# Two weight loads a step earlier, and four parts of the second matmul placed by hand

## The chip, the cores and the metric

The kernel runs on one core of a Trainium2 chip (trn2). The metric is the device time of one execution in microseconds; the median of the runs counts. "The profile" is one profiled execution of the same program, with its own time.

## The reference

Causal attention with a forget gate over 8 batches, 8 heads, 576 positions and head dimension 64, followed by a two-layer block with SiLU on 4608 tokens of width 512:

```python
scores = q @ k.T / sqrt(D)
cum = cumsum(log(clip(f, 1e-4, 1)))
scores = where(causal, -1e9, scores + cum[:, None] - cum[None, :])
x = softmax(scores) @ v            # heads side by side: 4608 x 512
h = x @ w_in                       # 512 x 2048
out = (h * sigmoid(h)) @ w_out     # 2048 x 512, float32
```

## The kernel before

All five engines' instructions stand in an order that the program writes out by hand; nothing is rescheduled. An engine issues in that order and waits on semaphores, so an instruction that waits holds up everything behind it on its engine.

**Attention.** exp(cum differences) is split: the values v are multiplied by exp(half - cum) per key (`convert_v0` for the first 128 rows of a batch, L349, and `convert_v` for the rest, L423, both on GpSimd), the ones column gives the softmax sum, and the query's factor cancels. The first 128 rows of a batch are made by `turn0` (L294, q and k turned by TensorE into a "big" PSUM buffer, copied by ScalarE for q and by VectorE for k), `scores0` (L328, exp on ScalarE, L335), `mask0` (L344, the causal mask on VectorE), `out0` (L368, times v; the reciprocal and xq on VectorE, L377 and L383) and `back0` (L398, xq transposed, copied by ScalarE into x, L399). The other 448 rows go by units of a batch and a pair of heads, two units to a pass m of the last loop: `scores` (L469, exp L474 and L480), `mask` and `mask_tail` (L486, L492), `attend` (L516, L525; reciprocal L533, xr L534) and `back` (L558, xr transposed, copied by VectorE, L561 and L564; from the fourth pass on by a DMA transpose).

**The two-layer block.** Tokens are taken in groups g: the first 128 rows of batches 0 to 3 are group 0 (512 columns), those of batches 4 and 5 group 1 (256), of 6 and 7 group 2 (256); then the rest. M1, `m1_chunk` (L577), makes one of 16 chunks of 128 hidden units of a group by four matmuls: ScalarE's tanh (`th`, L585) and VectorE's `gt` (L586) evacuate it. M2, `m2_part` (L622), is a quarter of the second matmul of a tile of 128 tokens: four matmuls of 128x512 into `po`, needing one of the four w_out loads; after the fourth, ScalarE makes `osb` (L632), of which there are four buffers, and SyncE stores it (L601).

**PSUM.** Four single-bank buffers ("big") serve `tp`, `tx`, `hp`, `po` and `dn`; a `po` holds one for its whole tile. Two double-bank buffers serve the scores.

**The order.** `fill(us)` places M1 chunks and M2 parts for about so many planned microseconds between the steps of attention; `wanted` chooses between the two (M2 only once `open2["w"]` is set), `step(kind)` places one, `at["left"]` carries the rest of a plan over. `two_more(4)` and `two_more(6)` do the first rows of two batches with fills between them. After them comes the loop over m, whose passes place fills (`slot`, `rest`) up to a planned total.

**The queues.** `load_qk0`, most of `load_v0`, `load_w_in` and `load_w_out` are issued by GpSimd, whose order is shared with its conversions and casts. SyncE issues the other loads, the DMA transposes and the stores, and starts its loads behind `after`, which waits for the second w_out load.

Of the kernel before, what the change touches and what calls it, by code (L numbers as in the profile page):

```python
# [18 lines left out]
def kernel(  # L19
# [177 lines left out]
    def load_w_in(i):  # L197
        c0, c1 = i * DFF // WQ, (i + 1) * DFF // WQ
        nc.gpsimd.dma_start(out=w_in_bf[:, :, c0:c1], in_=w_in_v[:, :, c0:c1])
# [106 lines left out]
    def ban0(b):  # L306
        sc = psc.tile([P, 2, NP, P], FP32, name="sc", tag="sc")
        for i in range(2):
            nc.tensor.matmul(  # L309
                sc[:, i, :, :].rearrange("p a t -> p (a t)"),  # L310
                lhsT=ident_bf[:, :],
                rhs=ban[:, :, :].rearrange("p a t -> p (a t)"),
                start=True,
                stop=False,
            )
        return sc

    def scores0(b, sc=None):
        t = qT0.pop(b)
        fresh = sc is None  # L320
        u = upool.tile([P, 2, NP, P], BF16, name="u", tag="u")
        u0[b] = u
        if fresh:
            sc = psc.tile([P, 2, NP, P], FP32, name="sc", tag="sc")
        for p in range(NP):
            for i in range(2):
                r = slice(i * D, (i + 1) * D)
                nc.tensor.matmul(  # L328
                    sc[:, i, p, :],
                    lhsT=kT0[b][r, p, :],  # L330
                    rhs=t[r, p, :],
                    start=fresh,
                    stop=fresh or p == NP - 1,
                )
        nc.scalar.activation(  # L335
            out=u[:, :, :, :].rearrange("p i a t -> p (i a t)"),
            in_=sc[:, :, :, :].rearrange("p i a t -> p (i a t)"),
            func=ACT.Exp,
            scale=scale,
        )  # L340
# [7 lines left out]
    def convert_v0(b):  # L348
        nc.gpsimd.tensor_tensor(  # L349
            out=v0[b][:, :, :],  # L350
            in0=vf0.pop(b)[:, :, :],
            in1=w_bf[:, 0, b * H : (b + 1) * H, None].to_broadcast([P, H, D + 1]),
            op=ALU.mult,
        )
# [215 lines left out]
    def m1_chunk(g, fc):  # L570
        w = GW[g]
        if fc == 0:
            gts[g] = gpools[g % 3].tile([P, NFC, w], BF16, name="gt", tag=f"gt{g % 3}")
        gt = gts[g]
        hp = pbig.tile([P, w], FP32, name="hp", tag="big")
        for cc in range(NCC):
            nc.tensor.matmul(  # L577
                hp[:, :],
                lhsT=w_in_bf[:, cc, fc * P : (fc + 1) * P],
                rhs=xcols(g, cc),  # L580
                start=(cc == 0),
                stop=(cc == NCC - 1),
            )
        th = tpool.tile([P, w], BF16, name="th", tag="th")
        nc.scalar.activation(out=th[:, :], in_=hp[:, :], func=ACT.Tanh, scale=0.5)  # L585
        nc.vector.scalar_tensor_tensor(  # L586
            out=gt[:, fc, :],
            in0=th[:, :],
            scalar=1.0,
            in1=hp[:, :],  # L590
            op0=ALU.add,
            op1=ALU.mult,
        )
# [10 lines left out]
    def m2_part(g, tb, part):  # L604
        gt = gts[g]
        last = g == NG - 1 and tb == GW[g] // P - 1
        if last:
            if part % 2 == 0:
                pos[g, tb] = pbig.tile([P, DM // 2], FP32, name="po", tag="big")
            m0 = part // 2 * DM // 2  # L610
            m1 = m0 + DM // 2
            fcs = range(part % 2 * NFC // 2, (part % 2 + 1) * NFC // 2)
            done = part % 2 == 1
        else:
            if part == 0:
                pos[g, tb] = pbig.tile([P, DM], FP32, name="po", tag="big")
            m0, m1 = 0, DM
            fcs = range(4 * part, 4 * part + 4)
            done = part == 3
        po = pos[g, tb]  # L620
        for fc in fcs:
            nc.tensor.matmul(  # L622
                po[:, :],
                lhsT=gt[:, fc, tb * P : (tb + 1) * P],
                rhs=w_out_bf[:, fc, m0:m1],
                start=(fc == 0),
                stop=(fc == NFC - 1),
            )
        if done:
            store(len(stores) - 3)  # L630
            osb = opool.tile([P, m1 - m0], FP32, name="osb", tag="osb")
            nc.scalar.activation(out=osb[:, :], in_=po[:, :], func=ACT.Copy, scale=0.5)  # L632
            for n, (r, b, s0) in enumerate(rows_of(g, tb)):
                t0 = b * S + s0
                q_ = nc.scalar if last and n == 1 else nc.sync
                stores.append((q_, out[t0 : t0 + r.stop - r.start, m0:m1], osb[r, :]))
# [45 lines left out]
    at = {"m1": 0, "m2": 0, "left": 0.0}  # L682
    ready: set[int] = set()
    open2 = {"w": False}
# [4 lines left out]
    def wanted(a, c):  # L689


        g1 = M1[a][0] if a < len(M1) else NG
        g2 = M2[c][0] if c < len(M2) else NG
        can1 = g1 in ready and not (M1[a][1] == 0 and g1 > g2 + lag["g"])
        can2 = open2["w"] and c < len(M2) and g2 < g1
        if can1 and can2 and lag["parts"]:
            return 2 if sum(M2_OF[:g1]) - c > lag["parts"] else 1
        if not can1 or not can2:
            return 1 if can1 else 2 if can2 else 0
        a0, c0 = begin.get(g1, (M1[a][1], c)) if M1[a][1] else (0, c)  # L700
        c1 = sum(M2_OF[:g1])
        f1 = (M1[a][1] - a0 + 0.5) / (NFC - a0)
        f2 = (c - c0 + 0.5) / max(1, c1 - c0)
        return 1 if f1 <= f2 else 2

    def step(force=0):

        a, c = at["m1"], at["m2"]
        want = wanted(a, c)
        if not want:  # L710
            return None
        g1 = M1[a][0] if a < len(M1) else NG
        g2 = M2[c][0] if c < len(M2) else NG
        can1 = g1 in ready and not (M1[a][1] == 0 and g1 > g2 + lag["g"])
        can2 = open2["w"] and c < len(M2) and g2 < g1
        kind = force if (force == 1 and can1) or (force == 2 and can2) else want
        if kind == 1:
            if M1[a][1] == 0:
                begin[g1] = (0, c)
            m1_chunk(g1, M1[a][1])  # L720
            at["m1"] += 1
            t = 4 * (GW[g1] / 2.4 + 2.5)
        else:
            m2_part(*M2[c])
            at["m2"] += 1
            t = 4 * (DM / 2.4 + 2.5)
        return t
# [20 lines left out]
    def fill(us_, least=0, ends=(0, 0)):  # L748

        left = us_ + at["left"]  # L750
        kinds = plan(left)
        kinds += [0] * (least - len(kinds))
        if any(ends) and kinds:
            if 2 not in kinds:
                kinds[0] = 2
            n1, n2 = len(kinds) - kinds.count(2), kinds.count(2)
            e0 = 1 if ends[0] else 0
            e1 = 1 if ends[1] and n2 > e0 else 0
            inner = n2 - e0 - e1
            n = n1 + inner  # L760
            mid = [2 if (x + 1) * inner // n > x * inner // n else 1 for x in range(n)]
            if inner and mid[-1] == 2 and e1 and not e0:
                mid = mid[::-1]
            kinds = [2] * e0 + mid + [2] * e1
        for k in kinds:
            t = step(k)
            if t is None:
                at["left"] = 0.0
                return
            left -= t / 1000  # L770
        at["left"] = left
# [13 lines left out]
    gpool = ctx.enter_context(tc.tile_pool(name="gpool", bufs=1))  # L785
    first_pool = tc.tile_pool(name="first", bufs=1)
    gpools = [first_pool.__enter__(), gpool, gpool]
    convert_v0(0)
    load_w_in(0)
    turn0(1, 0)  # L790
    turn0(1, 1)
    turn0(2, 0)
# [3 lines left out]
    out0(0, apart=True)  # L796
    turn0(3, 0)
    scores0(2, ban0(2))
    convert_v0(2)
    load_w_in(1)  # L800
    turn0(3, 1)
    bans = ban0(3)
    out0(1, apart=True)
# [53 lines left out]
    def two_more(b):  # L857
        for x in range(2):
            turn0(b + x, 0)
            turn0(b + x, 1)  # L860
        fill(1.2, 2)
        for x in range(2):
            scores0(b + x)
            mask0(b + x)
        fill(2.6 if b == 4 else 3.4, 3)
        out0(b)
        fill(0.6, 1)
        out0(b + 1)
        fill(0.8, 2)
        back0(b, on_act)  # L870
        fill(0.6, 1)
        back0(b + 1, on_act)
        fill(0.6, 1)

    fill(5.9)
    two_more(4)
    ready.add(1)
    fill(3.0)
    open2["w"] = True
    begin[M1[at["m1"]][0]] = (M1[at["m1"]][1], at["m2"])  # L880
    fill(6.0)
    two_more(6)
    ready.add(2)
    fill(4.2)
# [75 lines left out]
    for m in range(NQ):  # L960
# [16 lines left out]
        if m > 0:  # L977
            if m % 2 == 0:
                b = m // 2 - 1
# [79 lines left out]
```

## Time and profile before

| | us |
|---|---|
| median of 3 runs | 340.43 |
| lowest, highest | 340.33, 341.62 |
| profiled execution | 340.98 |
| its span, first to last instruction | 339.2 |
| TensorE busy | 330.6 |
| ScalarE, VectorE, GpSimd busy | 216.9, 193.6, 137.4 |

The granted TensorE clock is 1.00 throughout. Busy times are shares of the whole span; what one engine waits for in one place is read from the waits, the chain and the timeline. Line numbers of the profile before are those of the kernel before; in the changed kernel the lines behind the edit are the same up to L870.

### The profile page before, as it was taken

How to read it: one execution, taken by the hardware profiler on the slowest of the kernel's cores; microseconds unless marked ns; L12 is line 12 of the kernel's file. 1: busy time of each engine (PE TensorE's matmuls, PEld its weight loads, DVE VectorE, ACT ScalarE, POOL GpSimd, SP SyncE). 2: the span in 40 equal slices, each digit the busy share in tenths (PEclk: the TensorE clock that was granted, in tenths of full speed). 3: DMA queues.
4: the chain of work that ended last, by engine and by line, in shares of the span. 5: the costliest groups of instructions: out<-in, count | busy, mean ns of one | idle time of the engine just before them, and what ended most of it. 6: DMA issues, size and time to landing. Idle time of an engine off the chain costs nothing.

```text
span 339.2 us, 10025 instructions
## 1 busy us (share of the span) xinstructions
PE 330.6 (97%) x4132; PEld 222.4 (66%) x4132; DVE 193.6 (57%) x425; ACT 216.9 (64%) x389; POOL 137.4 (41%) x217
## 2 busy tenths in 40 slices
PE   7999899999999999999999999999999999999995
PEld 3745565577656768857766896867776676555654
DVE  4668935267567556655656865684672558334330
ACT  5766635677867767848748784875776485444431
POOL 8895417636756455454374434536060000000000
PEclk9999999999999999999999999999999999999999
DMA  8999999999999799999998969989763210001012
GB/s 151 190 185 222 182 210 155 199 236 177 156 190 236 117 215 134 163 211 151 168 178 172 142 130 175 134 168 165 148 123 66 56 37 33 31 33 64 33 62 63
DMA packets 144702, 48.00 MB, mean 142 GB/s; under 512 B 133328, under 2 KB 139728, under 8 KB 144656
## 3 DMA queue, kind: packets, MB, share of 16 engines
q1 hardware_dynamic: 115088, 36.60, 59.5%
q0 software_dynamic: 29408, 10.62, 26.6%
q8 instruction: 32, 0.52, 0.7%
q10 hardware_dynamic: 160, 0.13, 0.2%
q14 instruction: 14, 0.11, 0.1%
HBM read 36.85 MB, written 9.44 MB: 136 GB/s over the span
## 4 chain that ended last, share of the span: by engine, by line
PE 92%; ACT 2%; DVE 2%; DMA 2%; issue 1%; POOL 0%; POOLq 0%
PE hp L577 35%; PE po L622 24%; PE pr L648 12%; PE sc L469 7%; PE dn L516 6%; PE dn L525 3%; PE tp L294 2%; DMA qkb<-in_k_dram 2%; DVE u L344 1%; DVE gt L586 1%; ACT x L399 1%; PE sc L309 1%; PE sc L328 1%; ACT u L335 1%; PE tx L558 0%
## 5 line engine op out<-in xcount | busy, mean ns | idle before, releaser
L585 ACT ACTIVATE th<-hp 128x384 bf16<-128x384 f32 (+2 forms) x208 | 96.0, 469 | 78.7 <-PE hp L577 75.8
L586 DVE SCALAR_TENSOR_TENSOR gt<-th,hp 128x384 bf16<-128x384 bf16 (+2 forms) x208 | 107.1, 522 | 67.3 <-ACT th L585 58.5
L577 PE MATMUL hp<-x,w_in_bf 128*128 128x384 bf16 (+2 forms) x704 | 122.1, 321 | 1.5 <-ACT x L399 0.9
L577 PEld LDWEIGHTS <-w_in_bf 128*128 128x128 bf16 x832 | 79.4, 98 | 50.6 <-issue 1.8
L622 PE MATMUL po<-w_out_bf,gt 128*128 128x512 bf16 (+1 forms) x400 | 93.8, 371 | 0.0
L480 ACT ACTIVATE u<-sc 128x1024 bf16<-128x1024 f32 (+1 forms) x96 | 74.4, 814 | 6.4 <-PE sc L469 6.4
L622 PEld LDWEIGHTS <-gt 128*128 128x128 bf16 x400 | 37.6, 98 | 32.5 <-issue 0.2
L410 POOL CAST qkb<-qf 128x384 bf16<-128x384 f32 x32 | 16.7, 522 | 95.1 <-DMA qf<-in_q_dram 94.8
L648 PE MATMUL pr<-w_out_bf,gt 64*128 64x256 bf16 x768 | 46.0, 269 | 0.0
L158 POOL DMA_DIRECT2D qkb<-in_k_dram x56 | 43.8, 784 | 0.7 <-issue 0.7
L648 PEld LDWEIGHTS <-gt 64*128 64x128 bf16 x768 | 38.5, 94 | 2.8
L423 POOL TENSOR_TENSOR vp<-vf,w_bf 128x520 bf16<-128x520 f32 (+1 forms) x32 | 34.1, 1069 | 10.3 <-DMA vf<-in_v_dram 9.0
L632 ACT ACTIVATE osb<-po 128x512 f32<-128x512 f32 (+1 forms) x25 | 14.6, 583 | 22.6 <-PE po L622 19.5
L469 PE MATMUL sc<-qkT 64*128 64x128 bf16 (+1 forms) x640 | 27.9, 206 | 0.4 <-ACT u L480 0.3
L469 PEld LDWEIGHTS <-qkT 64*128 64x128 bf16 x640 | 19.9, 94 | 8.6 <-issue 6.5
L486 DVE TENSOR_TENSOR u<-u,tri 128x768 bf16<-128x768 bf16 x32 | 19.4, 605 | 10.5 <-ACT u L480 10.5
L474 ACT ACTIVATE ut<-sc 128x640 bf16<-128x640 f32 x32 | 22.5, 702 | 1.7 <-PE sc L469 1.3
L516 PEld LDWEIGHTS <-u 128*128 128x128 bf16 x576 | 20.6, 98 | 2.9
L516 PE MATMUL dn<-vp,u 128*128 128x65 bf16 x384 | 21.8, 194 | 0.0
L534 DVE TENSOR_TENSOR xr<-dn,rec 128x448 bf16<-128x448 f32 x32 | 20.0, 624 | 1.1
L516 PE MATMUL dn<-v,u 128*128 128x65 bf16 x192 | 20.0, 194 | 0.0
L577 PE MATMUL hp<-xt,w_in_bf 128*128 128x256 bf16 x128 | 16.6, 273 | 0.0
(72 smaller groups left out, 228.1 us busy)
## 6 DMA issues: line engine op xcount, KB each, us to landing
out_dram<-osb SPq DMA_DIRECT2D x32, 256.0 KB, 3.5
vf<-in_v_dram SPq DMA_DIRECT2D x26, 256.0 KB, 5.5
qf<-in_q_dram SPq DMA_DIRECT2D x64, 96.0 KB, 3.4
qkb<-in_k_dram POOLq DMA_DIRECT2D x56, 48.0 KB, 4.6
w_in_bf<-in_moe_w_in_dram POOLq DMA_DIRECT2D x4, 512.0 KB, 6.8
w_out_bf<-in_moe_w_out_dram POOLq DMA_DIRECT2D x4, 512.0 KB, 8.7
vf<-in_v_dram POOLq DMA_DIRECT2D x6, 256.0 KB, 10.3
qkb<-in_q_dram POOLq DMA_DIRECT2D x8, 128.0 KB, 5.5
```

The costliest lines, as they stand in the source:

```text
L158: nc.gpsimd.dma_start(out=t2[:, NR + 1 : NX, j * D : (j + 1) * D], in_=k[b, head(p, j), P:SM, :].rearrange("(c p) d -> p c d", p=P),)
L423: nc.gpsimd.tensor_tensor(out=vbf[b][r, c, :, :], in0=vst[b][c][r, :, :], in1=w_bf[r, c + 1, b * H : (b + 1) * H, None].to_broadcast([n, H ...
L469: nc.tensor.matmul(sc[:, i, o : o + q1 - q0], lhsT=kt, rhs=t[r, q0:q1], start=True, stop=True)
L474: nc.scalar.activation(out=ut[:, :, 0:3:2, :].rearrange("p k i t -> p i k t"), in_=sc[:, :, T0 : T0 + (NM + 1) * ST].rearrange("p i (k t) ...
L480: nc.scalar.activation(out=u[:, :, c * SM : c * SM + w], in_=sc[:, :, 0:w], func=ACT.Exp, scale=scale)
L516: nc.tensor.matmul(dn[:, i * NR + c - 1, :], lhsT=u[:, i, o : o + P], rhs=vals(kb, i), start=(kb == 0), stop=(kb == c),)
L534: nc.vector.tensor_tensor(out=xq[:, :, p % 2, :], in0=dn[:, :, 0:D], in1=rec[:, :, None].to_broadcast([P, NGR, D]), op=ALU.mult,)
L577: nc.tensor.matmul(hp[:, :], lhsT=w_in_bf[:, cc, fc * P : (fc + 1) * P], rhs=xcols(g, cc), start=(cc == 0), stop=(cc == NCC - 1),)
L585: nc.scalar.activation(out=th[:, :], in_=hp[:, :], func=ACT.Tanh, scale=0.5)
L586: nc.vector.scalar_tensor_tensor(out=gt[:, fc, :], in0=th[:, :], scalar=1.0, in1=hp[:, :], op0=ALU.add, op1=ALU.mult,)
L622: nc.tensor.matmul(po[:, :], lhsT=gt[:, fc, tb * P : (tb + 1) * P], rhs=w_out_bf[:, fc, m0:m1], start=(fc == 0), stop=(fc == NFC - 1),)
L648: nc.tensor.matmul(pos[g, tb][y], lhsT=gt[r, fc, tb * P : (tb + 1) * P], rhs=w_out_bf[r, fc, y * DM // 2 : (y + 1) * DM // 2], start=(half ...
```

## The change

Three edits. On GpSimd the first w_in load is issued ahead of `convert_v0(0)` instead of behind it, and the second ahead of `convert_v0(2)`. In `two_more(4)`, after `back0(5)`, the fill (which had nothing to place, since group 0's M1 was done and group 1 not yet declared ready) is replaced by one M2 part, and M2 is opened there. Between `two_more(4)` and `two_more(6)` ten steps are placed by name (seven M1 chunks, three M2 parts), the carried rest is set to zero, and the fill that follows is planned at 2.6 instead of 3.0 + 6.0 us.

```diff
+    load_w_in(0)
     convert_v0(0)
-    load_w_in(0)
     turn0(1, 0)
...
     scores0(2, ban0(2))
+    load_w_in(1)
     convert_v0(2)
-    load_w_in(1)
     turn0(3, 1)
...
         back0(b + 1, on_act)
-        fill(0.6, 1)
+        if b == 4:
+            open2["w"] = True
+            step(2)
+        else:
+            fill(0.6, 1)
 
     fill(5.9)
     two_more(4)
     ready.add(1)
-    fill(3.0)
-    open2["w"] = True
+    for kind in (1, 1, 2, 1, 1, 2, 1, 1, 1, 2):
+        assert step(kind) is not None
+    at["left"] = 0.0
     begin[M1[at["m1"]][0]] = (M1[at["m1"]][1], at["m2"])
-    fill(6.0)
+    fill(2.6)
     two_more(6)
```

TensorE's order then differs in this way (x256 and x512 are the columns of one matmul; four make a chunk or a part). Before: 7 chunks of M1 in a row behind `back0(5)`, then parts and chunks mixed, 6 parts and 10 chunks in all ahead of `two_more(6)`. After: 1 part, 2 chunks, 1 part, 2 chunks, 1 part, 3 chunks, 2 parts, 1 chunk, 1 part, 1 chunk: 6 parts and 9 chunks. The fills behind it place what follows differently: in the first pass of the loop a part more and no chunk or part between the attends and the second pass's scores; in the fourth pass one part fewer ahead of the attends, so that four chunks stand in a row there. From the fifth pass on the orders are the same.

## The prediction

> **What bounds the kernel now.** First the page's engine line:
>
> ```profile
> PE 330.6 (97%) x4132; PEld 222.4 (66%) x4132; DVE 193.6 (57%) x425; ACT 216.9 (64%) x389; POOL 137.4 (41%) x217
> ```
>
> TensorE does the same matmuls before and after, so only its idle time can move: 339.2 - 330.6 = 8.6 us, of which 3.8 us (the windows view) lie after 288 us. The built orders differ only up to about 107 us. Next, who waited for whom, TensorE alone, 38.5 to 288 us (us in total, times, longest):
>
> ```profile
> PE hp L577 <- ACT x L399: 0.9, 1, 0.9
> PE sc L469 <- ACT u L480: 0.3, 1, 0.3
> ```
>
> Little is left there. The chain of waits, 28 to 40 us, shows where the 0.9 us comes from (start, us, what):
>
> ```profile
> 29.04 0.92 ACT u L335
> ...
> 29.99 2.96 DVE u L344 x2
> 32.95 1.79 DVE gt L586 x3
> ...
> 37.78 0.59 ACT x L399
> ...
> 38.42 1.69 PE hp L577 x14
> ```
>
> VectorE sets the pace here, not TensorE: two masks, three evacuations, then the copy of the second group's x, for which its M1 waits. Last, GpSimd's timeline, and the DMA queues in the windows view (last two columns: share, GB/s):
>
> ```profile
> 10.28 1.05 POOL L349 TENSOR_TENSOR v<-vf,w_bf 128x520 bf16<-128x520 f32 x1 [0.91 <-issue]
> 11.28 0.80 POOL L199 DMA_DIRECT2D w_in_bf<-in_moe_w_in_dram  x1
> ...
> 29.89 2.51 POOL L349 TENSOR_TENSOR v<-vf,w_bf 128x520 bf16<-128x520 f32 x2 [4.04 <-DMA vf<-in_v_dram]
> ```
> ```profile
> 12.00:13.00 1.00, 1.00 (x25) 0.67 (x21) 0.93 (x5) 1.00 (x2) 0.98 (x2) 1.00 0.61 126
> 13.00:14.00 1.00, 1.00 (x26) 0.65 (x24) 0.34 (x1) 0.77 (x2) 1.00 (x2) 1.00 0.73 65
> 14.00:15.00 1.00, 1.00 (x18) 0.56 (x12) 0.74 (x2) 0.71 (x1) 0.98 (x3) 1.00 1.23 204
> ```
>
> GpSimd sits idle 0.91 us before the first conversion, and the transfers slacken between 12 and 14 us because no w_in is queued yet.
>
> **The two w_in loads.** GpSimd is free at 9.38 (7.53 + 1.85, the v loads), so the first issue (0.80) runs 9.38 to 10.18 instead of at 11.28, and the conversion still starts at 10.28, as its weights are ready at 10.14. Cost nothing; if it did start late, it has 0.45 us until out0(0)'s matmuls at 11.78. Conversion 1 comes 0.8 us earlier, w_in(1) is issued at 12.35 instead of 14.12, conversion 2 stays at 13.15. Conversion 3 still waits for its v (issued 8.45, landing 6.2 us later, 14.7), so GpSimd's later issues gain only 0.2 us. TensorE never waited for w_in. What can be gained is the slack: (204 - 126) + (204 - 65) = 217 KB at 204 GB/s, 1.06 us by which the queue's later transfers land earlier.
>
> Who needs that? Conversions 4 and 5 wait for v (4.04 us idle) and run beside the masks of 29.99: two masks take 2.96 us there, but 1.85 us (row at 52.86) beside no conversion. One us earlier, conversion 4 is over when the masks start; conversion 5 (v at 30.78 - 1.0) covers the first alone. The second takes 0.93 instead of 1.54 us: VectorE's chain is 0.6 us ahead at 32.95. Followed through the evacuations, xq, the last M1 and the copy, x is ready at about 37.94 instead of 38.37. **B: -0.45 us**; bounds 0 (no lead) and -0.75 (all waits 33 to 36.5 us, 0.67 us by their rows, and the second-order rest).
>
> GpSimd against VectorE has a rule. In these rows both slow down and neither stands still: a mask beside conversions took 1.50 us against 0.93, while the conversion beside it took 1.50 against 1.05. The Trainium skill (SBUF — State Buffer, "Who interferes with whom") says a VectorE instruction with two SBUF inputs and a GpSimd instruction that reads SBUF exclude each other, and the later one fully blocks. By it conversion 5, from 29.9, would hold both masks back to 31.9 and 32.8, B would be -0.1 and the sum +0.5. The trace does not bear a full block out: the first mask, begun 0.10 us after a conversion of 1.05 us, ended at 31.49, not at 31.88.
>
> **The first part in the gap.** TensorE ends back0(5)'s transposes at 37.48. The part (four 128x512 matmuls, 0.86 us by the row of po) needs w_out(0), landed at 24.32 + 9.0 = 33.3, and a PSUM buffer: in the built order that of chunk 13, evacuated at 36.94 + 0.62. So it runs 37.62 to 38.48, and M1 begins at 38.48 instead of 38.42. **A: -0.80 us.** The other three parts need w_out(1), (2), (3), landed at 35.9, 38.4 and 41.5; they come at 39.4, 41.1 and 43.3, cover 1.8 us or more. Fewer chunks stand between the second group's start and two_more(6), which starts about 1.4 us earlier; its q, k (45.0 at the latest) and v conversions (52.8 against a need at about 54) still hold.
>
> **What the new order makes late.** Walked with PSUM buffers as built and durations of the trace:
>
> - **C: -0.26 us.** In the first unit's piece, chunk 1 of the next head's scores waited for ScalarE (0.25 at 65.53). Now two M1 chunks instead of one precede it (0.44 more), and the wait goes. Bounds 0 and -0.41.
> - **D: +0.14 us.** The third turn0 in two_more(6) takes the buffer of an M1 chunk two tiles back; evacuation needs 1.47 us from a chunk's start (38.42 to 39.89), and 1.39 us passes. Bounds 0 and +0.3.
> - **E: +0.95 us.** After the second unit's attends the built order has no filler any more: scores (0.65 us), then back(0)'s transposes. Before, M1 and M2 (1.3 us) stood between. These are VectorE's rows before, attends ending at 71.68:
>
> ```profile
> 70.34 0.75 DVE L586 SCALAR_TENSOR_TENSOR gt<-th,hp 128x256 bf16<-128x256 bf16 x2 [0.33 <-ACT th L585]
> 71.03 0.20 DVE L533 RECIPROCAL rec<-dn 128x7 f32<-128x7 f32 x1
> ...
> 72.13 0.62 DVE L534 TENSOR_TENSOR xr<-dn,rec 128x448 bf16<-128x448 f32 x1
> ```
>
> xr is ready 1.07 us after the attends: a wait of 0.5 by itself. In the new ScalarE order an osb now stands ahead of the two th, which delays them by 0.48 (106.25 to 106.73, osb to th), the evacuations and xr likewise: 1.60 - 0.65 = 0.95. Queued behind the transposes on TensorE are the M2 part and three chunks; nobody else needs them. Bounds +0.45 and +1.1.
> - **F: +0.58 us.** In the fourth QUAD pass an M2 part ahead of the attends has gone earlier and four M1 chunks in a row (2.61 us) fill all four buffers. The attends take the first chunk's buffer, whose th waits behind three exps and the osb (103.47 + 0.48 + 0.44 + 0.39 + 0.91 + 0.58 + 0.27 = 106.54), evacuated at 107.7, wanted at 107.16. Bounds +0.2 and +0.75.
>
> From about 107 us the order is as before, dense, so the sum stays to the end: -0.80 - 0.45 - 0.26 + 0.14 + 0.95 + 0.58 = **+0.16 us**. The profiled execution took 340.98 us, span 339.2 and 1.8 around it, 0.55 above the median of the runs, 340.43. So 341.1 profiled, and 340.6 as a median.
>
> **The rivals.**
> 1. The new waits do not come (ScalarE has room to catch up, or the buffers come free sooner): A to D alone, -1.37, 339.1 us; with B and C at their far bounds 338.7. For it: in passes m = 2 on, transposes after little filler waited only 0.05 us. Against: there one chunk and no osb stood in that place.
> 2. Slower: the fifth osb. The output pool has four buffers, so the osb of E writes over the first one, whose store is the first of four queued on SyncE at 66.70, behind a transpose, landing 3.5 us later: 70.2. ScalarE wants it about 2.2 us after scores at 67.2 to 67.6, so at 69.4 to 69.8. If SyncE's chain does not come 1 us earlier with the loads, ScalarE stands 0.4 to 0.8 us with the th and exps behind it; E becomes 1.35 (B absent) and the sum +1.0: 341.4 us. It decides once the store lands after 69.4. Against: SyncE's loads start when w_out(1) has landed, which B moves too.
> 3. The w_in lead does nothing, because the load of v(3) and the queue's own latency fill the gap: B = 0, the sum +0.6, 341.0 us.
>
> **How the numbers follow.** The forecast 0.50 (its own range 340.0 to 341.2), rival 1 0.22, rival 2 0.15, rival 3 0.08, both masks held back in full by conversion 5 (B = -0.1) 0.05, 340.9 us. About 0.5%, 1.7 us, is what a measurement can tell from no change: below 338.7 lies only the far end of rival 1, with some room for a gap that I have not seen (0.11); above 342.1 only rival 2 with E and F at their upper bounds, or a wait not in the list (0.11); within, 0.78. Range: 339.0 (rival 1) to 341.8 (rival 2 with F at 0.75 and D at 0.3).
>
> **What would show it.** In the changed profile: GB/s near 200 at 12 to 14 us; conversions 4 and 5 about 1 us earlier and the second L344 near 0.93 us; a po of L622 before the first 128x256 M1 and no 0.9 us wait on x; new TensorE waits on xr at L558 near 72 us and on gt at L516 near 107 us. A wait of po on w_out, a late conversion 0, or no new wait at L558 would prove the steps wrong; a total outside 339.0 to 341.8, the sum.

## The result and the profile after

| | before | after |
|---|---|---|
| median of 6 runs, us | 340.57 | 346.35 |
| lowest, highest | 340.33, 341.62 | 344.09, 348.44 |
| profiled execution, its span | 340.98, 339.2 | 348.44, 346.7 |
| ratio, 95% interval | 1 | 1.0157 (1.0123 to 1.0191) |

The change costs 5.8 us in these runs; the profiled execution of after is the longest of its six. A second set of ten runs of after, on another occasion, had a median of 342.57 us, from 341.31 to 347.23 (ratio 1.0059, 1.0021 to 1.0098): six lie between 341.3 and 342.7, four between 344.6 and 347.2. The ratio of the second set leaves out its longest run, which lies more than 1.5% above its shortest. So the kernel has two outcomes, and what decides between them is the main thing to explain.

TensorE's waits in after (us in total, times, longest):

```profile
PE dn L516 <- ACT osb L632: 3.6, 1, 3.6
...
PE hp L577 <- DVE gt L586: 1.1, 1, 1.1
...
PE tx L558 <- DVE xr L534: 0.6, 1, 0.6
PE po L622 <- DMA w_out_bf<-in_moe_w_out_dram: 0.5, 1, 0.5
PE dn L516 <- DVE gt L586: 0.4, 1, 0.4
```

The 0.9 us wait for x and the 0.3 us wait of sc are gone, as forecast; the waits for xr and gt are there, as forecast; and above them stands one that before does not have, 3.6 us of the second unit's attends for an osb. ScalarE's timeline (start, us, instruction, idle before and who ended it) gives the reason:

```profile
68.94 0.39 ACT L480 ACTIVATE u<-sc 128x256 bf16<-128x256 f32 x1
73.26 0.60 ACT L632 ACTIVATE osb<-po 128x512 f32<-128x512 f32 x1 [3.93 <-DMA out_dram<-osb]
```

This is the fifth osb. ScalarE could begin it at 69.33; it starts when a store has landed. In before the same osb comes later and waits for its own po alone, 0.48 us:

```profile
73.19 0.60 ACT L632 ACTIVATE osb<-po 128x512 f32<-128x512 f32 x1 [0.48 <-PE po L622]
```

The chain of waits in after names the store too, here with the time of the transfer:

```profile
67.43 0.86 ACT u L480
68.30 4.88 DMA out_dram<-osb
...
74.16 0.75 DVE gt L586 x2
```

The fifth osb takes the first one's buffer, whose store was issued at 68.30 and landed at 73.17. Until then po keeps its PSUM bank, and the attends need that bank: TensorE stands from 70.28 to 73.90. What follows is seen in the windows (us, busy time of PE, PEld, DVE, ACT, POOL, then PEclk, DMA share, GB/s):

```profile
70.00:74.00 4.00, 0.38 (x14) 0.29 (x11) 0.00 (x0) 0.74 (x2) 1.09 (x2) 1.00 1.24 292
74.00:78.00 4.00, 3.16 (x48) 2.38 (x49) 2.75 (x8) 2.34 (x4) 1.27 (x3) 0.61 1.17 205
78.00:82.00 4.00, 4.00 (x33) 2.33 (x33) 1.01 (x4) 1.02 (x3) 3.20 (x6) 0.54 1.29 190
```

The second of these windows in before:

```profile
74.00:78.00 4.00, 4.00 (x47) 2.61 (x45) 2.00 (x5) 3.95 (x7) 2.57 (x5) 1.00 1.19 175
```

The granted clock, 1.00 there in before, falls behind the wait; by the clock's own records it is 0.5 from 74.84 to 81.67 us. The Trainium skill (TensorE: Matmul & The Clock Gate, Part 1) says that the clock halves after an idle window of about 3.4 us and returns after a busy one, and that the windows run freely. The length agrees: 6.83 us are two steps of 3.41, and the fall stands 68.27 us, twenty such steps, behind the clock's first record. The idle window agrees only in part. Counted in these steps, the window that ended at 74.84 began at 71.43, and TensorE was busy for 0.94 us of it, behind the wait.

Step by step along the units, by the start of each unit's third exp (L474): after is 0.70 us ahead of before in the second unit and 5.78 behind in the third (6.5 us lost between), 6.14 behind in the ninth, and 7.41 behind from 215 us on. The last 1.27 is the wait of 1.1 in the first list. There a mask_tail (L492) on VectorE took 1.65 us, against 0.22 in before: it ended at 211.76, 0.09 us behind a conversion on GpSimd (L423). The second profile of after has no such wait, and before's order has one of 0.5 us there in two of its other profiles (w_in loads alone, first part alone). So it comes and goes with the run and is not put down to the change.

### The profile page after: what moved, and what is told of

Its sections match the earlier page's. It is cut to its first block, busy times and chain, and to the rows that moved or that the text cites. A ratio compares the mean times of both kernels' runs of the same rounds, so it can differ in the third digit from the quotient of the medians.

```text
span 346.7 us, 9995 instructions
## 1 busy us (share of the span) xinstructions
PE 332.0 (96%) x4101; PEld 224.4 (65%) x4132; DVE 194.6 (56%) x425; ACT 217.2 (63%) x389; POOL 137.8 (40%) x217
## 3 DMA queue, kind: packets, MB, share of 16 engines
HBM read 36.85 MB, written 9.44 MB: 134 GB/s over the span
## 4 chain that ended last, share of the span: by engine, by line
PE 83%; DMA 9%; DVE 3%; POOL 2%; issue 1%; ACT 1%; ACTq 0%; POOLq 0%
PE hp L577 30%; PE po L622 23%; PE pr L648 12%; PE sc L469 7%; PE dn L516 5%; DMA vf<-in_v_dram 5%; DMA w_out_bf<-in_moe_w_out_dram 3%; PE dn L525 3%; DMA out_dram<-osb 1%; PE wm L241 1%; PE tp L294 1%; DVE gt L586 1%; POOL v L349 1%; DVE ut L492 1%; POOL qkb L132 1%
## 5 line engine op out<-in xcount | busy, mean ns | idle before, releaser
L622 PE MATMUL po<-w_out_bf,gt 128*128 128x512 bf16 (+1 forms) x373 | 90.2, 372 | 2.6 <-issue 0.7
L158 POOL DMA_DIRECT2D qkb<-in_k_dram x56 | 43.8, 784 | 1.0 <-issue 0.7
L423 POOL TENSOR_TENSOR vp<-vf,w_bf 128x520 bf16<-128x520 f32 (+1 forms) x32 | 34.0, 1072 | 8.9 <-DMA vf<-in_v_dram 8.0
L486 DVE TENSOR_TENSOR u<-u,tri 128x768 bf16<-128x768 bf16 x32 | 20.8, 649 | 10.5 <-ACT u L480 10.3
L474 ACT ACTIVATE ut<-sc 128x640 bf16<-128x640 f32 x32 | 22.6, 705 | 2.5 <-PE sc L469 2.1
```

Source lines behind the costliest of these rows:

```text
L158: nc.gpsimd.dma_start(out=t2[:, NR + 1 : NX, j * D : (j + 1) * D], in_=k[b, head(p, j), P:SM, :].rearrange("(c p) d -> p c d", p=P),)
L423: nc.gpsimd.tensor_tensor(out=vbf[b][r, c, :, :], in0=vst[b][c][r, :, :], in1=w_bf[r, c + 1, b * H : (b + 1) * H, None].to_broadcast([n, H ...
L474: nc.scalar.activation(out=ut[:, :, 0:3:2, :].rearrange("p k i t -> p i k t"), in_=sc[:, :, T0 : T0 + (NM + 1) * ST].rearrange("p i (k t) ...
L486: nc.vector.tensor_tensor(out=x, in0=x, in1=tri[:, None, None, :].to_broadcast([P, 2, NR, P]), op=ALU.mult)
L622: nc.tensor.matmul(po[:, :], lhsT=gt[:, fc, tb * P : (tb + 1) * P], rhs=w_out_bf[:, fc, m0:m1], start=(fc == 0), stop=(fc == NFC - 1),)
```

## The experiments

The theory: the store lands after ScalarE wants the buffer; the wait is 3.6 us, and the clock behind it costs more. The rivals: the moved w_in loads push all later transfers back; or the new order of M1 and M2 costs the time by its other waits.

**A fifth buffer.**

```
...
- osb = opool.tile([P, m1 - m0], FP32, name="osb", tag="osb")
+ outs["n"] += 1
+ if outs["n"] == 5:
+     osb = upool.tile([P, m1 - m0], FP32, name="osb5", tag="u")
+ else:
+     osb = opool.tile([P, m1 - m0], FP32, name="osb", tag="osb")
...
```

> The fifth osb is taken from the pool of the u tiles instead of the output pool, so it need not wait for the first store; all else is as after. Theory (the fifth osb waits for the first store, 3.6 us of idle TensorE, and the half clock behind it costs 3.4 us more): the gap before the second unit's dn at 70.28 us is gone, the granted clock is 1.00 throughout, and the time is 346.3 - 3.6 - 3.4 = 339.3, between 339 and 341. Rival 1 (the moved w_in loads push the later transfers back by 1.5 us and that is the cost): 345 to 347. Rival 2 (the new order's other waits, 0.6 on xr at 76.5, 0.5 on w_out at 42.8, 0.4 on gt at 113.5 and 1.1 on gt at 212, are the cost): at most 2.6 us of the 5.8 are theirs, so at least 343.

341.33 us, ratio 1.0007 (0.9990 to 1.0024), clock 1.00. The time is above the forecast 339 to 341, but all the loss against before is gone with one buffer, and both rivals fall. The other waits are still there:

```profile
PE tx L558 <- DVE xr L534: 0.8, 1, 0.8
...
PE po L623 <- DMA w_out_bf<-in_moe_w_out_dram: 0.7, 1, 0.7
...
PE dn L516 <- DVE gt L586: 0.4, 1, 0.4
```

**Matmuls on zeros in the wait.**

```
...
  attend(n)
+ if m == 0:
+     idle = psc.tile([P, SM], FP32, name="idle", tag="sc")
+     for _ in range(17):   # 8 in the second kernel
+         nc.tensor.matmul(idle[:, :], lhsT=warm[:, 0:P], rhs=warm[:, :], ...)
  attend(n + 1)
...
```

> After, with 17 matmuls of 128x512 on zeros, into a scores buffer that nothing reads, between the first two units' attends: the wait of 3.6 us stays, but TensorE works through it (17 x 0.213 = 3.6 us). Theory with the clock: the granted clock stays at 1.00 behind the wait, and the time is 346.3 - 3.4 = 342.9, between 342.3 and 344. Rival (the clock of 0.5 at 74.8 to 81.7 us has another cause than the idle stretch, or it costs nothing on the path): 346, with the clock at 0.5 again.

344.97 us (343.27 to 345.23), ratio 1.0113 (1.0079 to 1.0147), clock 0.998 or more in every run. The 17 matmuls cost their 3.6 us whether the store is late or not (in the profiled run it landed at 69.43, in time), so this kernel should sit at the fifth buffer's 341.33 plus 3.6 = 344.9, as its median does; its four runs spread by 2 us. Against after's first set, whose six runs all lie above 344, that leaves 1.0157 - 1.0113 = 0.0044 of 341, an estimate of 1.5 us, for the clock. The forecast, 342.3 to 344, failed: the 3.4 us of the theory were too many.

> After, with 8 of the 17 idle matmuls (1.7 us) between the two attends: the wait of 3.6 us is half filled, some 1.9 us of it stay idle. Theory (a stretch idle for most of 3.6 us halves the clock, a shorter one does not): clock 1.00 behind it, and the time between 343.3 and 345, as with 17, or less where the store lands early. Rival (any idle stretch lowers the clock, or the wait itself grew): 346.

345.01 us, but from 341.53 to 346.98: five runs at 341.5 to 343.6, five at 346.4 to 347.0. The profiled run is one of the late ones. ScalarE's osb, TensorE and the clock there:

```profile
72.45 0.60 ACT L632 ACTIVATE osb<-po 128x512 f32<-128x512 f32 x1 [3.84 <-DMA out_dram<-osb]
```
```profile
69.40 1.89 PE L1025 MATMUL idle<-warm 128*128 128x512 bf16 x8
73.10 0.19 PE L516 MATMUL dn<-v,u 128*128 128x65 bf16 x1 [1.80 <-ACT osb L632]
```
```profile
74.00:78.00 4.00, 2.96 (x37) 2.06 (x34) 2.27 (x7) 2.33 (x3) 2.16 (x4) 1.00 1.13 208
```

Half of the wait is filled, and in this run the clock stays at 1.00. From the second to the third unit it loses 3.9 us, the wait and little else; after's profiled run lost 6.5 in the same place. Read there, the clock cost after's run about 2.5 us. By the ninth unit the two have lost 5.6 and 6.8, and the difference is down to 1.2: with the full clock TensorE met waits of 0.5 and 1.0 us for gt on the way, in after one of 0.4. The forecast for the time failed: the late runs took 346.4 to 347.0 and not at most 345. In this profile waits for gt add 1.5 us ahead of attends and 1.3 ahead of M1. The other four late runs have a mean clock of 0.995 or 0.989. One step of 3.41 us at half clock takes 0.005 off the mean, so the clock fell in them too, but the mean doesn't say where. That a half-filled wait keeps the clock up is shown for one run alone.

**One half of the change alone.** First the w_in loads (before, with load_w_in(0) ahead of convert_v0(0) and load_w_in(1) ahead of convert_v0(2)):

> Before, with only the two w_in loads moved. Theory: no time by itself; SyncE's first store is issued at 68.3 instead of 66.7 us and lands near 73, just when the fifth osb is wanted (73.2), so 340.3 to 341.2. Rival 1 (the later transfers are the cost): 343 to 346.

341.36 us, ratio 1.0002 (0.9982 to 1.0022): nothing. In its profile the first store was issued at 68.81 and landed at 73.96. ScalarE stood 1.71 us before the fifth osb, about the last 1.3 of them for the store (its po was ready at 72.7), and TensorE 0.54 at 76.5 us for the exps behind it. So before's order runs the same race at a lower price. Then the M2 parts (after, with the loads back in their places):

> After, with the w_in loads back where before has them: only the M2 parts' new places. Theory: the first store is issued at 66.7 and lands at 70.2 as before, ScalarE wants the fifth osb from 69.4 on, so a wait of about 0.8 us is left, too short for the clock to fall: 340.6 to 341.8, clock 1.00. If the store is as late here as in after (so that the new places of M2 delay it, not the w_in loads): 345 to 347. Rival 2 (the new order's waits by themselves): 343 to 346 with the clock at 1.00.

346.04 us, ratio 1.0130 (1.0072 to 1.0188), three runs at 345.8 to 346.7 and one at 343.03. The loss belongs to the order of M1 and M2, but the sum that gave 0.8 us of wait failed: the store was issued at 68.31 here as well, landed at 73.18, and the attends waited 3.6 us. The clock was 0.5 for 3.41 us, one window instead of two, and the loss from the second unit to the third 4.2 us.

**The same order, the stores elsewhere.** After, with the stores issued earlier, and before, with them issued later:

```
...
  ready.add(2)
  fill(4.2)
+ store(len(stores))
...
```

> After, with the first four stores put ahead of the fourth unit's load and transpose on SyncE, where their four osb have been written since 62.5 us. Theory (first store too late on SyncE): the first store is issued near 65.5 and lands before 69.7, when ScalarE wants the fifth buffer; no idle TensorE there, clock 1.00, and the time of the fifth buffer's run, 341.3 (340.3 to 342); the fourth transpose is issued some 1.6 us later, which costs nothing as its unit's scores come after 80 us. Rival (the buffer is not freed by the landing but by something that stands later in the program): 346 as after.

341.39 us, ratio 1.0009 (0.9993 to 1.0025). The first store was issued at 65.11 and landed at 68.24; the fifth osb ran at 70.16 without a wait. The fourth transpose came later than thought harmless: scores waited 0.5 us for qkT.

In the second kernel the first slot stores nothing:

```
+ opened: list = []
...
- n = len(stores)
+ n = len(stores) if opened else 0
+ opened.append(1)
...
```

> Before, in its own order of TensorE, with only the first four stores moved on SyncE from ahead of the fifth unit's load and transpose to behind them (their first issue near 73 instead of 66.7 us). Theory: the wait belongs to the store's place and not to the change; the first store lands near 76.5, ScalarE wants the fifth osb at 73.2 and stands for 3 us, TensorE with it, and the time is 343 to 346, the lower end if the clock stays. Rival (only the new order makes the wait costly): 341, within 0.5%.

343.70 us, ratio 1.0081 (1.0051 to 1.0111): before's order of TensorE loses time as well when its stores come late. In the profiled run, at 341.82 its shortest, ScalarE and TensorE wait for the store as in after, TensorE for less:

```profile
74.33 0.60 ACT L632 ACTIVATE osb<-po 128x512 f32<-128x512 f32 x1 [3.02 <-DMA out_dram<-osb]
```
```profile
74.98 0.60 PE L577 MATMUL hp<-x,w_in_bf 128*128 128x256 bf16 x4 [0.88 <-ACT osb L632]
```

The six runs at 343.7 us and above have a mean clock of 0.995 or less, the four shorter ones 0.998 or more; none of the six was profiled, so the length of their wait isn't seen.

**After once more.**

> After itself once more, beside the same runs of before as the experiments. Theory: the length of the wait and of the slow clock differ from run to run with the landing of the first store, so times spread from 343 to 348.5 with a median near 346; in the profiled run the scores' exps of the third unit come later against before by the wait (up to 3.6 us), by about 0.5 to 2.5 us for the clock, and by nothing else, and from there to the end at most 1.5 us are added, by the wait for gt at the fourth step (0.4 to 1.1) and the one near 212 us (0 or 1.1). Rival (a constant cost of the new order, whatever the store does): the same time in all runs within 1 us.

342.57 us, from 341.31 to 347.23, which fits the two outcomes and no constant cost; the forecast spread, 343 to 348.5 with a median near 346, failed, since six of the ten runs came in time. All four late runs, like the six of the first set, have a mean clock of 0.995 or less; of the six short ones five have 0.998 or more. So the long times and a fall of the clock come together. The profiled run, 341.56, is one without the wait, so the terms of it could not be read there. It shows the other side of the race: the first store, issued at 66.56, landed at 69.95, and ScalarE came for the buffer at 70.03:

```profile
69.75 0.39 ACT L480 ACTIVATE u<-sc 128x256 bf16<-128x256 f32 x1
70.03 0.60 ACT L632 ACTIVATE osb<-po 128x512 f32<-128x512 f32 x1
```

**Attempts at a faster kernel.** A chunk of M1 behind the second unit's attends, `slot(0.8, 1)` at the first step, with the fifth buffer and with the early stores:

> The fifth-buffer kernel, and one chunk of M1 put back behind the second unit's attends at the first step, where after has none. Theory of the prediction's term E (the transposes wait 0.8 us for xr because nothing stands between): the wait on xr at 73 us is gone, and the time falls by 0.6 to 0.8 to 340.6. Rival (that wait only takes the place of one that comes later on ScalarE): 341.3 as without it.

340.89 us, ratio 0.9996 (0.9984 to 1.0008). The wait on xr falls from 0.8 to 0.4. This profile is also the plainest evidence of the cause: its first store was as late as after's, issued at 68.62 and landed at 73.00, and with a buffer of its own the fifth osb ran at 69.50 without a wait:

```profile
69.50 0.62 ACT L637 ACTIVATE osb<-po 128x512 f32<-128x512 f32 x1
```

> Both at once: the four stores early, and the chunk of M1 behind the attends. Theory: neither wait is left, clock 1.00, the time as with a fifth buffer and the chunk, 340.6 (339.8 to 341.4), so no slower than before. Rival (the chunk only moves the wait): 341.3.

341.25 us, ratio 0.9996 (0.9966 to 1.0026). Neither beats before. The first part alone (before, with `step(2)` in place of the fill behind back0(5)):

> Before, with only the first M2 part moved into the place of the chunk of M1 that waits 0.94 us for x at 38.4; the other parts follow where before has them, and the w_in loads stay. The prediction's term A: 0.8 us less than before, 340.2, as long as the second part does not wait for w_out. Rival (the gain is given back in a wait for w_out or behind ScalarE): as before, 341.0. If the fifth osb comes so much earlier that it waits for the first store: 342 or more, with a wait at the second unit's dn.

340.94 us, ratio 0.9993 (0.9969 to 1.0016): the rival's price. TensorE's waits show where the gain went:

```profile
PE po L622 <- DMA w_out_bf<-in_moe_w_out_dram: 1.6, 1, 1.6
PE sc L469 <- DMA qkT<-qkb: 1.4, 1, 1.4
```

It stands 1.6 us for w_out at 43.35, and its scores reach a transpose 1.4 us too early. Last, after with the fifth buffer and the chunk behind the attends, and its later parts put back by two chunks of M1:

> The fifth buffer and the chunk behind the attends, and the fourth and later M2 parts of the first tile two chunks of M1 (0.87 us) further back, so that they do not wait for the last w_out load (0.8 us at 43 us in that kernel's trace). Theory: that wait goes and 0.5 to 0.8 us are won: 340.3, ratio 0.998. Rival (the place that sets the end comes later, on ScalarE's exps): 340.9 as without it.

340.94 us, ratio 1.0006 (0.9987 to 1.0024). The wait for w_out is gone from the profile, and that run was 1.26 us ahead of before until 204.73 us; there it met the chance wait of 1.1 us. Over the runs nothing was won.

## Why the prediction was wrong

**The forecast's sum holds for a kernel without the wait.** It said +0.16 us in the profiled sum; the fifth buffer's profile is 0.20 behind before from the ninth to the twenty-second unit, its median within 0.1% of before. But its terms did not all hold, and their errors cancelled:

- *The queue's later transfers land 1.06 us earlier.* The first step was right: w_in(0) was issued at 9.30, and the queue moved 177 and 185 GB/s at 12 to 14 us, against 126 and 65. The next step failed. Nothing of the lead reached w_in(2), which was issued at 18.06 as in before and landed at 26.16 against 25.95. Conversions 4 and 5 began at 29.84 against 29.89, and w_out(3) landed at 42.78 against 41.49. B was 0, the outcome of rival 3; what took up the lead was not followed. The later landing of w_out(3) is not the moved loads: without them it landed at 42.80 (M2 parts alone) and 43.30 (first part alone).
- *Both masks.* They ended at 30.2 and 31.7, earlier than before, for a reason not put down to the change: the first began at 29.52, ahead of the conversions.

```profile
29.52 0.69 DVE L344 TENSOR_TENSOR u<-u,tri 128x1024 bf16<-128x1024 bf16 x1 [0.23 <-ACT u L335]
30.44 1.24 DVE L344 TENSOR_TENSOR u<-u,tri 128x1024 bf16<-128x1024 bf16 x1 [0.22 <-ACT u L335]
```
```profile
29.84 2.74 POOL L349 TENSOR_TENSOR v<-vf,w_bf 128x520 bf16<-128x520 f32 x2 [3.97 <-DMA vf<-in_v_dram]
```

  Here the prediction misread its rows. With 0.69 us for a mask by itself and 1.05 for a conversion, each ends its own time behind the end of the other, less about 0.15 us. The conversion begun at 29.84 ends at 31.13 (30.21 + 1.05 - 0.13), the second mask at 31.67 (31.13 + 0.69 - 0.15); in before the first mask ends at 31.49 (30.95 + 0.69 - 0.15). The full block by the Trainium skill (SBUF — State Buffer, "Who interferes with whom") is what these rows show. The prediction denied it because it took 0.93 us for a mask alone, from the row at 52.86, where GpSimd was casting (52.76 to 54.87).
- *A.* The part ran at 36.39 and the wait for x went. The step "cover 1.8 us or more" for the other parts failed: w_out(3) came later and the M2 parts earlier, and 0.5 to 0.8 us of the 0.8 were given back.
- *C* is right: no wait of sc in after.
- *D* cannot be told apart: no wait for that buffer is in the list.
- *E* and *F* came where they were forecast, at 0.6 to 0.8 instead of 0.95, and 0.4 instead of 0.58 us. E's own figures give 0.90 (1.07 + 0.48 - 0.65), and rival 1's far bound comes to 338.6, not 338.7; neither would have moved the forecast out of its range.

**The step that failed is the price of rival 2.** Its mechanism, place and point of decision were right: the fifth osb, the first of four stores on SyncE, ScalarE at 69.4 (69.33). The forecast's sum gave the wait nothing, and rival 2 gave it 0.4 to 0.8 us, because the landing was taken as before's, 66.70 + 3.5 = 70.2, and only its lead was thought uncertain. Where the store came late, the wait was 3.6 us. The profiles give the landing as follows:

| kernel | store issued | landed | took |
|---|---|---|---|
| later parts put back | 65.74 | 69.31 | 3.6 |
| matmuls on zeros, 17 | 66.10 | 69.43 | 3.3 |
| after, once more | 66.56 | 69.95 | 3.4 |
| before | 66.70 | 70.14 | 3.4 |
| fifth buffer | 67.35 | 70.53 | 3.2 |
| matmuls on zeros, 8 | 67.38 | 72.37 | 5.0 |
| after | 68.30 | 73.17 | 4.9 |
| M2 parts alone | 68.31 | 73.18 | 4.9 |
| first part alone | 68.32 | 71.85 | 3.5 |
| fifth buffer, chunk behind | 68.62 | 73.00 | 4.4 |
| w_in loads alone | 68.81 | 73.96 | 5.2 |

Two things were missed. The issue moves by 3.1 us from profile to profile, with and without the moved loads. In all eleven it stands 4.9 to 5.3 us behind the landing of one and the same load of v (61.72 in before, 63.05 in after, 61.66 in after once more): GpSimd's conversion of that v, its casts of q and k, and the fourth transpose come between. It doesn't follow w_out(1), to which the prediction tied it: that landed at 36.37 in after and 36.85 in after once more, whose store came earlier. What moves the load of v was not followed. And the transfer does not slide with the issue: issued up to 67.35 it took 3.2 to 3.6 us, from 67.38 on 4.4 to 5.2 in five of six. So in these profiles the store came either just in time or 3 to 4 us late for after's order. GpSimd's loads of k (L158) are on the way with the store in the late cases, but in before as well, and where the stores stand elsewhere on SyncE they took 3.1 us (issued at 65.11) and 2.4 (at 71.86). So what holds the late ones back is open. Before hardly feels it, since it wants the buffer at 73.2; bringing M2 forward took away 3.9 us of slack that no wait in its profile showed.

**The clock was not in the sum at all.** In before it stayed at 1.00 over a wait of 0.94 us, in after it fell behind one of 3.6. By the losses between the second and the third unit (4.2 and 6.5 us, against 3.9 with the clock at 1.00) it cost from 0.3 us (M2 parts alone) to about 2.5 us (after); by the ninth unit (5.7 and 6.8, against 5.6) from 0.1 to 1.2. These are estimates from one profile each. The run with the clock at 1.00 took 346.53 us, 1.1 of it the chance wait, so most of the loss is the wait and the waits behind it, and the clock is the smaller part.

## What to carry to other kernels

When an instruction is brought forward, write down for each buffer that it takes when that buffer was free before, not only when the instruction waited: slack that nobody used is in no list of waits. Price a missed transfer by what it does when it is late, among the transfers that are queued then, and not by its duration when it was on time. And read a change of several per cent between runs of one kernel as a race: look for the two events whose order differs.

## What was not expected of the hardware

The granted clock also fell without a long idle stretch. In the second profile of after (windows, columns as above):

```profile
16.00:18.00 2.00, 0.95 (x15) 0.66 (x16) 1.36 (x4) 1.49 (x4) 2.00 (x5) 1.00 1.24 202
18.00:22.00 4.00, 3.82 (x11) 1.49 (x13) 0.98 (x2) 1.41 (x3) 3.99 (x6) 0.61 1.13 147
```

It was 0.5 from 18.90 to 22.32 us, 3.41 us, though TensorE's longest gap in the ten us before it was 0.6 us. It had been busy for half of the two us before; the fifth buffer's profile has the same 0.94 of 2.00 us there and kept 1.00. The phase of the 3.41 us steps does not explain it: in the step that ended at 18.90 TensorE was busy for 2.00 us, and in the step from 70.61 to 74.03 of the kernel with 8 matmuls on zeros for 1.61, and there the clock stayed. No share of busy time that the profiles show tells the two apart. The execution still took only 341.56 us.
